# Forward transforms of a fused SSM convolution and feed-forward kernel: the small-tile matmuls' columns laid end to end over whole PSUM banks

## Chip, cores and metric

The kernel runs on one core of a Trainium2 chip, in one launch. The metric is the device time in microseconds: the median of three runs before the change is 1106.26 us (1106.08 to 1107.27). The engines are called PE (matmul), PEld (its weight loads), DVE (vector), ACT (scalar), POOL and SP (here mostly issuers of DMAs).

## What is computed

```python
x = A_u                                   # 1 x 2048 x 576
xn = layernorm(x)
return x + ssm_conv(xn, ...) + ffn(xn, w1, w2)

# ssm_conv: per channel d a response of 2048 taps, then a long convolution
dt = exp(log_dt);  P = exp(dt * A * l)                  # A complex, 576 x 128; l = 0..2047
K = real(sum_n C * P * (dt * B))                        # response, 576 x 2048
y = irfft(rfft(pad(u)) * rfft(pad(K)))[:2048] + u * Dskip
# ffn
out = silu(xn @ w1) @ w2                                # 576 -> 4608 -> 576
```

## The kernel before, in words

Two streams of work share the engines. The main stream is the feed-forward (`ffn`): for each half of the rows, for nine chunks of w1 and w2 and two blocks of 512 rows, `up` multiplies 128 columns of w1 into a bank of PSUM (L343 to L345; ACT applies SiLU on L351 and casts on L352, DVE forms the low part on L354) and `down` multiplies back with w2 (L369; DVE adds each bank to the running sum, L373). Operands are split into a high and a low part, so that three matmuls take the place of one. DVE and ACT also split the weights (L305, L328; L303, L326).

The side stream is the convolution: a first part makes the response and stores it to HBM (`d1k`), and a transform of the inputs (`d1u`); then `spectral` does the rest of the forward transforms, the products and most of the way back; `tail` reads its result (`d2`) for a last transform and adds it to the outputs. `weave` (L33) threads the side stream into the main one: a generator of the side yields a number between 0 and 1 (`marks` on L963 places `spectral` between 0.597 and 0.86), and its next piece is emitted when the feed-forward has come so far. Within that, the kernel's planner (L1133) orders each engine's queue by what it reckons to be ready; `tc.high_priority()` puts an instruction ahead, and `behind(ins)` forbids that an instruction is placed ahead of `ins` on the same engine.

`spectral` works on 16 pairs of frequencies, p = 0 to 15, each with a response operand and an input operand of 128 rows by two parts by 576 columns:

- `load_k`, `load_u`, `load_m` issue from POOL the loads of the response (five DMAs, L761 and L763), the input (L754) and the matrices (L771, L774).
- `halves` (L777): three operations of DVE make the two operands of the response (tile `k`, one buffer) from the loaded `kw` (two buffers).
- `visit` (L787): one operand is transformed by matmuls of 64 rows by 32 columns on eight small tiles of the array (two row groups, four column groups), L796. Its result is four banks of PSUM, [row group, column half], of which each holds 288 of 512 columns. One set of four banks (`psb`) serves all visits and `back`. There are 32 visits, a response and an input for each pair.
- `clear` (L813): ACT copies the four banks out in two copies of 576 columns (L817).
- `response` and `inputs` (L802, L819): after the response's visit ACT makes the swapped copies `kb` and `ka` (L808 to L810); after the input's visit DVE makes the complex products and their low parts (L827 to L834), ACT the high parts (L833).
- `back` (L836): twelve matmuls of 128 by 128 (L847), two copies out, two stores to `d2` from POOL (L852).

The loop of L877 emits for each p, a step of the stage each: the next response, the next input, `back`.

Of the kernel before, what the change touches and what calls it, by code (L numbers as in the profile page):

```python
# [19 lines left out]
P = 128  # L20
# [23 lines left out]
def kernel(  # L44
# [699 lines left out]
    def spectral():  # L744

        uv = d1u.rearrange("(m p r) d -> p r m d", m=2, r=P)
        kv = d1k.rearrange("(m p r) d -> p r m d", m=2, r=P)
        cwt = kl.tile([P, 16, 3], F32, name="cwt", bufs=1)
        nc.sync.dma_start(cwt, cw)
        us, ks, mats, kab, ys = {}, {}, {}, {}, {}  # L750

        def load_u(p):
            t = kl.tile([P, 2, D], F32, tag="u", name="u")
            nc.gpsimd.dma_start(t, uv[p])  # L754
            us[p] = t

        def load_k(p):
            if p > 15:
                return
            w = kl.tile([P, 3, D], F32, tag="kw", name="kw")  # L760
            nc.gpsimd.dma_start(w[:, 0:2], kv[p])  # L761
            for r in range(4):
                nc.gpsimd.dma_start(w[32 * r:32 * r + 32, 2], kv[p, 32 * (r ^ 1):32 * (r ^ 1) + 32, 1])  # L763
            ks[p] = w

        def load_m(p, i):
            if p > 15:
                return
            if i:
                t = kl.tile([P, 2, 2, P], F32R, tag="mm", name="mm")  # L770
                nc.gpsimd.dma_start(t, cm23[:, p, 1:].rearrange("r (k w) c -> r k w c", w=2))  # L771
            else:
                t = kl.tile([P, P], F32, tag="m2", name="m2")
                nc.gpsimd.dma_start(t, cm23[:, p, 0])  # L774
            mats[p, i] = t

        def halves(p):  # L777
            if p > 15:
                return
            w, t = ks[p], kl.tile([P, 2, D], F32, tag="k", name="k", bufs=1)  # L780
            ks[p] = t
            c = cwt[:, p]
            nc.vector.scalar_tensor_tensor(w[:, 2], w[:, 2], c[:, 0:1], w[:, 1], op0=ALU.mult, op1=ALU.add)
            for m in range(2):
                nc.vector.scalar_tensor_tensor(t[:, m], w[:, 2], c[:, 1 + m:2 + m], w[:, 0], op0=ALU.mult, op1=ALU.add)  # L785

        def visit(p, t, name):  # L787

            banks = psb.tile([P, 2, 2, 512], F32, tag="psb", name=name)
            last = pins["pe"]  # L790
            for n, (h, g) in enumerate(((0, 1), (0, 0), (1, 1), (1, 0))):
                gs = slice(64 * g, 64 * g + 64)
                for o in range(4):
                    os = slice(32 * o, 32 * o + 32)
                    with tc.high_priority(), behind(last):
                        last = nc.tensor.matmul(banks[os, g, h, :HD], mats[p, 0][gs, os], t[gs, o % 2, h * HD:(h + 1) * HD],  # L796
                                                start=True, stop=True, tile_position=(64 * g, 32 * o),
                                                skip_group_check=True).ins
            pins["pe"] = last
            return banks  # L800

        def response(p):  # L802

            kas = [kl.tile([P, D], F32, tag="ka", name="ka") for _ in range(2)]
            clear(visit(p, ks.pop(p), "pk"), kas)
            for g in range(2):
                ka, kb = kas[g], kl.tile([P, D], F32, tag="kb", name="kb")
                nc.scalar.mul(kb[:64], ka[64:], -1.0)  # L808
                nc.scalar.copy(kb[64:], ka[64:])
                nc.scalar.copy(ka[64:], ka[:64])  # L810
                kab[2 * p + g] = ka, kb

        def clear(banks, dsts):  # L813

            with tc.high_priority():
                for g in range(2):
                    nc.scalar.copy(dsts[g].rearrange("p (h d) -> p h d", h=2), banks[:, g, :, :HD])  # L817

        def inputs(p):  # L819

            uts = [kl.tile([P, D], F32, tag="ut", name="ut") for _ in range(2)]
            clear(visit(p, us.pop(p), "pu2"), uts)
            for g in range(2):
                ka, kb = kab.pop(2 * p + g)
                y = kl.tile([P, D], F32, tag="y", name="y", bufs=1)
                y2 = kl.tile([P, D], F32, tag="y2", name="y2", bufs=1)
                nc.vector.tensor_mul(y, uts[g], ka)  # L827
                nc.vector.tensor_mul(y2[:64], uts[g][64:], kb[:64])
                nc.vector.tensor_mul(y2[64:], uts[g][:64], kb[64:])  # L829
                nc.vector.tensor_add(y, y, y2)  # L830
                ys[2 * p + g] = [kl.tile([P, D], F32R, tag=n, name=n, bufs=2) for n in ("yh", "yl")]
                yh, yl = ys[2 * p + g]
                nc.scalar.copy(yh, y)  # L833
                nc.vector.tensor_sub(yl, y, yh)  # L834

        def back(p):  # L836
# [3 lines left out]
            for g in range(2):  # L840
                mk = mats[p, 1][:, g]
                parts = ys.pop(2 * p + g)
# [8 lines left out]
            for g in range(2):  # L851
                nc.gpsimd.dma_start(d2.rearrange("(p k) d -> k p d", k=32)[2 * p + g], yos[g])  # L852

        def load_u2(p):
            if p < 16:
                load_u(p)
# [280 lines left out]
```

## Time and profile before

| | |
|---|---|
| median of three runs | 1106.26 us |
| the profiled execution | 1106.58 us |
| its span, first to last instruction | 1104.8 us |
| granted clock of PE, mean | 1.000 |
| first visit, last matmul of `back` | 671.8 us, 976.7 us |
| small-tile matmuls of the visits, two groups (response, input) | 512 + 512 instructions |
| DMA share in the stage from 669 to 985 us | 0.49 |

A row of a timeline gives the start and the length in microseconds, engine, line, operation, the tile written and the tiles read, rows x columns of the stationary operand, the moving operand's shape and how many were merged into the row; in brackets stands the engine's idle time before it and what ended it. Matmuls are pipelined: what one costs is the distance between starts, not its length. A row of a table of stretches has start and end, length, the busy time (instructions) of PE, PEld, DVE, ACT and POOL, the granted clock, DMA share and GB/s. A row of groups has busy time, mean ns of one, idle time before and its releasers.

### The profile page before, as it was taken

To read this page: it belongs to the slowest core of one execution; us is meant where nothing else is said; L and a number is where in the kernel's file an instruction comes from. 1 tells how busy PE (TensorE), PEld (TensorE's weight loads), DVE (VectorE), ACT (ScalarE), POOL (GpSimd) and SP (SyncE) were. 2 spreads that over 40 slices of the span, in tenths; PEclk is the share of its full clock that TensorE was granted. 3 is DMA by queue.
4 is the path that set the end of the run, shared out by engine and by line. 5 is a ranking of instruction groups with operands and counts; after the bars stand their busy time and mean duration, and the time that the engine had idled before them with its cause. 6 is when DMAs were issued, how large, how long until landed. Compare 5 with 4: busy or idle time off the path is not lost.

```text
span 1104.8 us, 23941 instructions
## 1 busy us (share of the span) xinstructions
PE 1095.5 (99%) x9807; PEld 961.4 (87%) x9807; DVE 891.6 (81%) x1431; ACT 659.5 (60%) x1030; POOL 136.2 (12%) x241
## 2 busy tenths in 40 slices
PE   9999999999999999999999999999999999999998
PEld 7999998999889898999989988788878878899887
DVE  7799899999999999989999836786868768653343
ACT  4565457676776776767766644766666656732220
POOL 1100000000000000011000023323232231000011
PEclk9999999999999999999999999999999999999999
DMA  9745512524253425265754166555546453248563
GB/s 265 208 123 155 150 58 62 121 72 118 85 108 107 99 76 137 62 157 154 198 150 96 55 143 211 163 160 173 166 145 188 151 168 122 67 144 209 135 173 107
DMA packets 174142, 150.23 MB, mean 136 GB/s; under 512 B 112288, under 2 KB 143792, under 8 KB 173904
## 3 DMA queue, kind: packets, MB, share of 16 engines
q1 hardware_dynamic: 156544, 93.77, 32.9%
q0 software_dynamic: 16736, 54.07, 15.6%
q8 instruction: 77, 1.26, 0.5%
q10 hardware_dynamic: 752, 0.85, 0.3%
q14 instruction: 33, 0.27, 0.1%
HBM read 104.13 MB, written 44.61 MB: 135 GB/s over the span
## 4 chain that ended last, share of the span: by engine, by line
PE 80%; DVE 10%; DMA 4%; ACT 2%; POOL 1%; issue 1%; DVEq 0%; ACTq 0%; POOLq 0%
PE po L369 35%; PE ph L343 30%; PE kp L708 3%; DMA kw<-d1k 3%; PE ph L344 3%; PE ph L345 2%; PE z L723 2%; DVE y L829 1%; PE pb L847 1%; DVE y L830 1%; PE pu L171 1%; DVE k L785 1%; DVE acc L373 1%; POOL kw L763 1%; DVE y L827 1%
## 5 line engine op out<-in xcount | busy, mean ns | idle before, releaser
L369 PE MATMUL po<-w2h,gh 128*128 128x288 f32 x1152 | 340.2, 297 | 2.2 <-DVE acc L373 2.1
L369 PE MATMUL po<-w2l,gh 128*128 128x288 f32 x1152 | 337.2, 295 | 0.0
L369 PE MATMUL po<-w2h,gl 128*128 128x288 f32 x1152 | 336.4, 296 | 0.2 <-DVE gl L354 0.2
L369 PEld LDWEIGHTS po<-w2h,gh 128*128 128x128 f32 x1152 | 215.7, 188 | 19.9 <-issue 8.4
L369 PEld LDWEIGHTS po<-w2l,gh 128*128 128x128 f32 x1152 | 215.5, 188 | 6.7 <-issue 1.9
L369 PEld LDWEIGHTS po<-w2h,gl 128*128 128x128 f32 x1152 | 214.9, 188 | 2.9 <-issue 0.9
L351 ACT ACTIVATE gf<-ph 128x512 f32<-128x512 f32 (+1 forms) x146 | 85.8, 588 | 186.9 <-PE ph L345 168.7
L354 DVE TENSOR_TENSOR gl<-gf,gh 128x512 fp32r<-128x512 f32 (+1 forms) x148 | 98.6, 671 | 87.3 <-ACT gh L352 86.7
L373 DVE TENSOR_TENSOR acc<-po,acc 128x288 f32<-128x288 f32 x288 | 126.0, 451 | 47.6 <-PE po L369 46.0
L343 PE MATMUL ph<-xh,w1h 128*128 128x512 f32 (+1 forms) x584 | 159.5, 389 | 0.0
L343 PE MATMUL ph<-xh,w1l 128*128 128x512 f32 (+1 forms) x584 | 159.2, 387 | 0.0
L343 PE MATMUL ph<-xl,w1h 128*128 128x512 f32 (+1 forms) x584 | 159.0, 387 | 0.0
L343 PEld LDWEIGHTS ph<-xl,w1h 128*128 128x128 f32 x584 | 107.0, 188 | 22.0 <-issue 1.4
L343 PEld LDWEIGHTS ph<-xh,w1l 128*128 128x128 f32 x584 | 106.7, 188 | 20.3 <-issue 0.5
L343 PEld LDWEIGHTS ph<-xh,w1h 128*128 128x128 f32 x584 | 103.6, 188 | 17.9 <-issue 0.9
L352 ACT CAST gh<-gf 128x512 fp32r<-128x512 f32 (+1 forms) x148 | 89.3, 610 | 19.4 <-PE po L369 16.4
L174 POOL DMA_DIRECT2D d1u<-u x32 | 17.4, 545 | 462.3 <-ACT u L173 460.4
L667 ACT ACTIVATE c<-th 128x1040 f32<-128x1040 f32 x36 | 38.7, 1075 | 46.0 <-DVE th L666 46.0
L833 ACT CAST yh<-y 128x576 fp32r<-128x576 f32 x32 | 21.5, 673 | 74.2 <-DVE y L830 71.0
L665 ACT ACTIVATE c<-th,magic 128x1040 f32<-128x1040 f32 x36 | 42.1, 1169 | 26.4 <-DVE C L688 23.3
L305 DVE TENSOR_TENSOR w1l<-w1r,w1h 128x640 fp32r<-128x640 f32 x72 | 57.0, 819 | 0.2
L344 PE MATMUL ph<-x,w1h 128*128 128x512 f32 (+1 forms) x146 | 56.6, 388 | 0.0
(195 smaller groups left out, 1757.7 us busy)
## 6 DMA issues: line engine op xcount, KB each, us to landing
w2r<-in_B_w_dram SPq DMA_DIRECT2D x72, 288.0 KB, 3.8
w1r<-in_B_w_dram SPq DMA_DIRECT2D x35, 512.0 KB, 3.9
d1u<-u POOLq DMA_DIRECT2D x32, 288.0 KB, 3.0
d1k<-stage SPq DMA_DIRECT2D x36, 256.0 KB, 5.1
u<-d1u POOLq DMA_DIRECT2D x16, 576.0 KB, 4.6
kw<-d1k POOLq DMA_DIRECT2D x16, 576.0 KB, 4.6
d<-yo POOLq DMA_DIRECT2D x32, 288.0 KB, 3.0
ys<-d SPq DMA_DIRECT2D x32, 288.0 KB, 6.0
```

The source lines that it names most:

```text
L305: pins["w1l"] = nc.vector.tensor_sub(l1, src, h1).ins
L343: nc.tensor.matmul(ph, w[:, kt, :], v[:, kt, a:e], start=n + kt == 0, stop=False)
L344: nc.tensor.matmul(ph, h1[:, 4, :], x4[:, a:e], start=False, stop=False)
L345: pins["pe"] = nc.tensor.matmul(ph, l1[:, 4, :], x4[:, a:e], start=False, stop=True).ins
L351: nc.scalar.activation(gf, ph, AF.Silu)
L352: pins["gh"] = nc.scalar.copy(gh, gf).ins
L354: pins["gl"] = nc.vector.tensor_sub(gl, gf, gh).ins
L369: pins["pe"] = nc.tensor.matmul(po[:, :HD], G[blk, t][g][:, js], W2[half, c, t][w][:, hs], start=n == 0, stop=n == 3 * FT - 1).ins
L373: nc.vector.tensor_add(acc[j][:, hs], po[:, :HD], acc[j][:, hs])
L665: nc.scalar.activation(c65, th, AF.Identity, bias=magic)
L667: nc.scalar.activation(c65, th, AF.Abs)
L708: mm = nc.tensor.matmul(dst, t[:, ch, :32], t[:, ch, 32:], start=begins and n == 0, stop=True, tile_position=(0, 32 * q), skip_group_check ...
```

## The change

The 32 operands (response 0, input 0, response 1, input 1, ...) are laid end to end, 576 columns each, and cut at every 512 columns, so that each visit fills its four banks wholly: 18 visits of 1024 columns for each row group, each with two to four pieces of up to three operands. A visit's pieces are 64 to 512 columns wide. ACT copies each piece out, both row groups at once, into tiles `ka` and `ut` that now hold both row groups of a pair. The swapped copies of the response are made after the visit in which the pair's input ends, in `products`, followed by the products of DVE, which now write in place into `kb` and `ut`. `halves` works in place in `kw`; the tile `k` is gone. The loads of the pair two on are issued right behind the visit that ends an operand; `halves` of a pair is emitted one visit after its buffer was freed, or in the same step where the next visit already needs it. `back` of a pair comes after the visit behind the one that ended its input. The small matrix `m2` has three buffers. The stage starts its first visit at 1.07 of its scale (1.05 before), with the loads of pair 1 moved up.

```diff
+        visits = [[] for _ in range((2 * D * NP + 1023) // 1024)]
+        for p in range(NP):
+            for kind in range(2):
+                c, at = 0, 2 * D * p + D * kind
+                while c < D:
+                    n = min(D - c, 512 - (at + c) % 512)
+                    visits[(at + c) // 1024].append((kind, p, c, n, (at + c) % 1024 // 512, (at + c) % 512))
+                    c += n
+        ends = [[(kind, p) for kind, p, c, n, _, _ in v if c + n == D] for v in visits]
...
         def halves(p):
...
-            w, t = ks[p], kl.tile([P, 2, D], F32, tag="k", name="k", bufs=1)
...
+                w, c = ks[p], cwt[:, p]
+                nc.vector.scalar_tensor_tensor(w[:, 2], w[:, 2], c[:, 0:1], w[:, 1], op0=ALU.mult, op1=ALU.add)
+                for m in range(2):
+                    nc.vector.scalar_tensor_tensor(w[:, 1 - m], w[:, 2], c[:, 1 + m:2 + m], w[:, 0],
+                                                   op0=ALU.mult, op1=ALU.add)
...
-        def visit(p, t, name):
-
-            banks = psb.tile([P, 2, 2, 512], F32, tag="psb", name=name)
+        def visit(v):
+
+            banks = psb.tile([P, 2, 2, 512], F32, tag="psb", name="pf")
             last = pins["pe"]
-            for n, (h, g) in enumerate(((0, 1), (0, 0), (1, 1), (1, 0))):
-                gs = slice(64 * g, 64 * g + 64)
-                for o in range(4):
-                    os = slice(32 * o, 32 * o + 32)
...
+            for kind, p, c, n, b, at in visits[v]:
+                for g in (1, 0):
+                    gs = slice(64 * g, 64 * g + 64)
+                    for o in range(4):
+                        os = slice(32 * o, 32 * o + 32)
+                        src = us[p][gs, o % 2] if kind else ks[p][gs, 1 - o % 2]
+                        with tc.high_priority(), behind(last):
+                            last = nc.tensor.matmul(banks[os, g, b, at:at + n], mats[p, 0][gs, os], src[:, c:c + n],
+                                                    start=True, stop=True, tile_position=(64 * g, 32 * o),
+                                                    skip_group_check=True).ins
             pins["pe"] = last
...
+            for kind, p, c, n, b, at in visits[v]:
+                held, tag = (uts, "ut") if kind else (kas, "ka")
+                if c == 0:
+                    held[p] = kl.tile([P, 2, D], F32, tag=tag, name=tag)
+                with tc.high_priority():
+                    nc.scalar.copy(held[p][:, :, c:c + n], banks[:, :, b, at:at + n])
+
+        def products(p):
+
+            ut, ka = uts.pop(p), kas.pop(p)
+            kb = kl.tile([P, 2, D], F32, tag="kb", name="kb", bufs=1)
             for g in range(2):
...
+                nc.scalar.mul(kb[:64, g], ka[64:, g], -1.0)
+                nc.scalar.copy(kb[64:, g], ka[64:, g])
+                nc.scalar.copy(ka[64:, g], ka[:64, g])
+            yield
             for g in range(2):
...
+                nc.vector.tensor_mul(kb[:64, g], ut[64:, g], kb[:64, g])
+                nc.vector.tensor_mul(kb[64:, g], ut[:64, g], kb[64:, g])
+                nc.vector.tensor_mul(ut[:, g], ut[:, g], ka[:, g])
+                nc.vector.tensor_add(ut[:, g], ut[:, g], kb[:, g])
+                yh, yl = (kl.tile([P, D], F32R, tag=n, name=n) for n in ("yh", "yl"))
+                nc.scalar.copy(yh, ut[:, g])
+                nc.vector.tensor_sub(yl, ut[:, g], yh)
...
         with behind(pins["gh"]):
             halves(0)
+        load_k(1)
+        load_m(1, 0)
+        load_u(1)
         load_m(0, 1)
...
+        yield 1.04
         halves(1)
...
+        load_m(2, 0)
+        steps = len(visits) + NP
...
+        for p in range(2, NP):
+            freed = (2 * D * (p - 2) + D - 1) // 1024
+            due.setdefault(min(freed + 1, 2 * D * p // 1024 - 1), []).append(p)
+        for v in range(len(visits)):
+            yield 1.07 + (2 - 1.07) * n / steps
+            n += 1
+            visit(v)
+            for kind, p in ends[v]:
+                if kind:
+                    load_u(p + 2)
+                    load_m(p + 3, 0)
+                else:
+                    load_k(p + 2)
+            done = [p for kind, p in ends[v] if kind]
+            for p in done:
+                for _ in products(p):
+                    pass
+            for p in due.get(v, ()):
+                halves(p)
+            for p in ready:
+                yield 1.07 + (2 - 1.07) * n / steps
+                n += 1
+                back(p)
                 load_m(p + 1, 1)
...
+            ready = done
```

More of the change, by code (lines that the diff above doesn't have):

```diff
@@ L761, in load_k @@
[L761 to L764, printed above, removed]
-        def load_m(p, i):
[L767 to L775, printed above, removed]
```

110 lines of the change are left out of this document (34 added, 76 removed).

## The prediction

> **What bounds the kernel now.** I read the page's busy table first, then the stretches, then the PE's own waits, then the timeline of one visit.
>
> ```profile
> span 1104.8 us, 23941 instructions
> ...
> PE 1095.5 (99%) x9807; PEld 961.4 (87%) x9807; DVE 891.6 (81%) x1431; ACT 659.5 (60%) x1030; POOL 136.2 (12%) x241
> ```
> ```profile
> 669.00:985.00 316.00, 313.65 (x2671) 261.80 (x2670) 234.56 (x361) 206.63 (x342) 80.64 (x144) 1.00 0.49 149
> 985.00:1105.00 120.00, 115.19 (x897) 100.31 (x896) 48.30 (x99) 24.27 (x42) 10.72 (x22) 1.00 0.62 161
> ```
> ```profile
> PE po L369 <- DVE acc L373: 2.1, 3, 0.7
> ```
>
> The first fence says that PE is busy for 99% of the span. A busy PE can hide overhead, so the stage of the change has to be read alone: 669 to 985 us, where PE is busy for 313.65 of 316 us at granted clock 1.00, DVE for 234.56 (74%), ACT for 206.63 (65%). The third fence has PE's waits in that stage: 2.1 us, for DVE's adds of the feed-forward. So PE is not waiting for the transform; it is full, and what changes the time here is the PE time that a visit costs, or a wait put into PE's queue. After 985 us PE is busy for 115.19 of 120 us, so a gain made earlier is carried to the end.
>
> ```profile
> 744.88 0.29 PE L369 MATMUL po<-w2l,gh 128*128 128x288 f32 x1
> 745.01 0.43 PE L369 MATMUL po<-w2h,gl 128*128 128x288 f32 x2
> 745.37 1.20 PE L796 MATMUL pk<-k,m 64*32 64x288 f32 x32
> 746.50 0.40 PE L369 MATMUL po<-w2h,gh 128*128 128x288 f32 x1
> 746.74 0.29 PE L369 MATMUL po<-w2l,gh 128*128 128x288 f32 x1
> ```
> ```profile
> 745.37 0.47 PE L796 MATMUL pk<-k,m 64*32 64x288 f32 x8
> ...
> 745.37 0.71 PE L796 MATMUL pk<-k,m 64*32 64x288 f32 x16
> ...
> 745.37 0.96 PE L796 MATMUL pk<-k,m 64*32 64x288 f32 x24
> ```
>
> These are one visit among feed-forward matmuls, and the same visit cut off by narrower windows. Feed-forward matmuls start 0.13 us apart, so the last one before the visit starts at 745.14. From there to 746.74 is 1.60 us, where two ordinary intervals would take 0.27: **a visit costs PE 1.33 us**. Inside it, 8, 16, 24 and 32 instructions take 0.47, 0.71, 0.96 and 1.20 us: each eight (one for each of the eight small tiles) take 0.243 us for 288 columns, 0.97 us for four eights. The other **0.36 us are fixed**: the switch into small tiles (0.10), out of them (0.11), and the fill and drain of the small tiles.
>
> **The change part by part.**
>
> ```profile
> L796 PE MATMUL pk<-k,m x512: 402/403/428, 671.8 to 955.6; 64*32 64x288 f32 x171
> ...
> L796 PE MATMUL pu<-u,m x512: 402/403/428, 678.9 to 961.3; 64*32 64x288 f32 x171
> ```
> ```profile
> L847 PE MATMUL pb<-yh,mm x128: 288/294/300, 699.7 to 976.7; 128*128 128x288 f32 x128
> ```
>
> *Matmuls.* Now: 1024 instructions, 32 a visit, 32 visits. After: 32 operands of 576 columns laid end to end, cut at every 512 columns, give 64 pieces (eight each of 512, 448, 384, 320, 256, 192, 128 and 64 columns) of 16 instructions: 1024 again, and 18,432 columns a row group, as now. Streaming stays at 32 x 0.97 = 31.1 us. Fixed: 32 x 0.36 = 11.5 us becomes 18 x 0.36 = 6.5 us. That is **5.0 us less on PE**, and all of it on the path.
>
> *Short pieces.* No visit shows a 64-column piece. The nearest other rows:
>
> ```profile
> 168.60 0.34 PE L708 MATMUL kp<-C 128*32 128x64 f32 x8
> ...
> 170.59 0.66 PE L369 MATMUL po<-w2h,gl 128*128 128x288 f32 x3
> ```
> ```profile
> 168.60:170.62 2.02, 2.02 (x128) 1.90 (x128) 1.00 0.04 8
> ```
>
> Here 128 instructions of 64 columns on four tiles take 1.99 us, 15.5 ns each. If that were a floor for each instruction, a piece of 16 would take at least 0.25 us, where 64 columns need 2 x 0.054 = 0.11 and 128 need 0.22: 0.14 + 0.03 us for each of eight, 1.4 us in all. The other end is nothing: inside the visit the first eight start within some 0.05 us (0.47 less the 0.43 of the longest one), 6 ns apart, and the four-tile row is itself near its streaming, 62 ns for a round of four against 54. I take 0.1 us, by the visit's row, and keep 1.4 for the range.
> [...]
>
> *Evictions, products, halves.*
>
> ```profile
> L667 ACT ACTIVATE c<-th 128x1040 f32<-128x1040 f32 x36 | 38.7, 1075 | 46.0 <-DVE th L666 46.0
> L173 ACT COPY u<-pu 128x288 f32<-128x288 f32 x64 | 24.3, 399 | 15.8 <-PE pu L172 15.8
> L817 ACT COPY ka<-pk 128x576 f32<-128x576 f32 x32 | 18.9, 640 | 3.3 <-PE pk L796 2.0 <-DVE y L827 1.3
> L809 ACT COPY kb<-ka 64x576 f32<-64x576 f32 x32 | 21.5, 671 | 0.4
> ```
> ```profile
> L373 DVE TENSOR_TENSOR acc<-po,acc 128x288 f32<-128x288 f32 x76 | 33.6, 452 | 7.0 <-PE po L369 6.6
> L354 DVE TENSOR_TENSOR gl<-gf,gh 128x512 fp32r<-128x512 f32 x39 | 26.7, 689 | 42.2 <-ACT gh L352 41.8
> L785 DVE SCALAR_TENSOR_TENSOR k<-kw,cwt 128x576 f32<-128x576 f32 x32 | 24.7, 812 | 0.0
> L829 DVE TENSOR_TENSOR y<-ut,kb 64x576 f32<-64x576 f32 x32 | 24.2, 756 | 0.5
> L305 DVE TENSOR_TENSOR w1l<-w1r,w1h 128x640 fp32r<-128x640 f32 x19 | 15.0, 821 | 0.1
> L328 DVE TENSOR_TENSOR w2l<-w2r,w2h 128x576 fp32r<-128x576 f32 x19 | 13.9, 752 | 0.0
> L783 DVE SCALAR_TENSOR_TENSOR kw<-kw,cwt 128x576 f32<-128x576 f32 x16 | 13.1, 817 | 12.1 <-DMA kw<-d1k 11.6 <-DVE y L829 0.2
> ```
>
> ACT evicts response and inputs with 64 copies of 576 columns now and with 64 copies of 128 to 1024 columns after, the same columns in all; from 399 and 640 ns a copy costs about 0.16 us and 0.84 ns a column, so the sum stays and the longest is about 1.0 us (the 1040-column row: 1.075). The six half copies of an operand pair (0.67 each, 4.0 us) move from behind the response's visit to behind the end of the inputs'. DVE does the same 13 operations a pair, 10 x 0.756 + 2 x 0.812 + 0.817 = 10.0 us, now in place. All of this is cost nothing, hidden under PE's 313.65 us while DVE and ACT have 26% and 35% of the stage free. If that cover went, PE would wait for the feed-forward's own work in the same in-order queues (L373, L354 on DVE, L351 and L352 on ACT).
>
> *Loads and waits.* POOL issues the same transfers. The load of the response two pairs on now waits for the visit that has read the buffer, not for DVE's halves:
>
> ```profile
> 749.57 0.72 POOL L761 DMA_DIRECT2D kw<-d1k  x1 [5.73 <-DVE k L785]
> 750.28 1.99 POOL L763 DMA_DIRECT2D kw<-d1k  x4
> ```
> ```profile
> DMA to landing us min/median/max: 3.1/4.2/9.4
> ```
>
> The last line is the landing of the transfers of `kw`. Behind the load in POOL's queue stand the input's load, the small matrix (a third buffer) and later the stores of back; POOL already sits through 5.73 us of such a wait, and is busy for only 80.64 of 316 us. The chain: visit 2.0, issue 2.7, landing 4.2 (at most 9.4), three halves 2.4 us: 11.3, at most 16.5. The time for it: 48 visits and backs now span 671.8 to 976.7; 34 start some 6 us later (1.07 of the stage's scale for 1.05) and save 5, so they come (305 - 11) / 33 = 8.9 us apart. For four pairs (6, 7, 14, 15) the freeing visit and the needing one are neighbours with one back between, 17.8 us; for the other ten there is a visit more. A visit that holds columns of both kinds waits for the later of them; behind it on PE stands all of the feed-forward. Since back follows three steps (26.7 us) after the visit, the longer chain of evictions, half copies, products (about 16 us of ACT and DVE) has room. I cost these at nothing. The first loads are only moved up in POOL's queue, ahead of a first visit that comes later. The single `kb` tile is free again a whole visit before its next use.
>
> Sum: 1104.8 - 5.0 + 0.1 = 1099.9 of span. The profiled execution took 1106.58, 1.78 more than its span, and stands 0.32 above the median: 1099.9 + 1.8 - 0.3 = **1101.4 us** beside 1106.26.
>
> **The rivals.**
>
> ```profile
> 671.77 0.67 PE L796 MATMUL pk<-k,m 64*32 64x288 f32 x2
> ...
> 673.29 1.20 PE L796 MATMUL pk<-k,m 64*32 64x288 f32 x30
> ```
> ```profile
> 899.22 0.40 PE L369 MATMUL po<-w2h,gh 128*128 128x288 f32 x1 [0.72 <-DVE acc L373]
> ```
> ```profile
> 747.07 0.75 DVE L830 TENSOR_TENSOR y<-y,y 128x576 f32<-128x576 f32 x1
> 747.73 1.54 DVE L785 SCALAR_TENSOR_TENSOR k<-kw,cwt 128x576 f32<-128x576 f32 x2
> 749.19 0.75 DVE L834 TENSOR_TENSOR yl<-y,yh 128x576 fp32r<-128x576 f32 x1
> ```
>
> 1. **It doesn't do what it says: visits fall apart.** The first visit now is two, 2 and 30 instructions with feed-forward between, since its order only forbids overtaking. Each break pays the fixed 0.36 us again. A visit now has up to three operands to wait for; nine breaks give back 3.2 us: 1104.6. Against it: the timeline shows no other visit broken so.
> 2. **A floor for each small instruction**, as under the short pieces: 1.3 us more than I take by the four-tile row, 1102.7. With a floor f, the pieces of 64, 128 and 192 columns lose 8 x (48 f - 0.65 us); the gain of 5.0 is gone at f = 27 ns, and the time is then that of before. Against it: the two rows above, 6 and 15.5 ns. [...]
> 3. **Slower: the halves come too late.** They stand in the code behind the ten products of the same step. If DVE keeps that order, the products start 6.2 us after the visit's start (visit 1.9, evictions 2.3, three half copies 2.0), and 7.56 + 2.44 us at the 72% that the feed-forward leaves (89.2 of 316 us are its own: 33.6 + 26.7 + 15.0 + 13.9) end at 20.1. It decides at 17.8: PE then stands 2.3 us at a visit. At the four narrow pairs that is 9.2 us, 1110.6; at all fourteen 32, 1133. Against it: the last fence shows DVE taking the halves of a later pair ahead of the last product of an earlier one, and PE's queue can put feed-forward ahead of a late visit.
> 4. **Bunching: DVE's or ACT's longer runs hold up L373.** Such a wait costs 0.72 us and some 0.1 for the refill; there are three. Nine in place of three cancel the gain; one for each of 16 pairs adds 13 x 0.8 = 10.4: 1111.8. For it: evictions, half copies and products now follow one visit; against it: no single operation but one copy gets longer.
>
> **How the numbers follow.** Forecast 1101.4: 0.62, since PE is full and the fixed cost is the same in every visit. Rival 1: 0.09; rival 2: 0.06; rival 3: 0.13; rival 4: 0.10. The forecast's own range is 1097.8 (the three waits and the broken visit's 0.8 us gone too) to 1104. A measurement of this kernel can tell about 0.2%, 2.2 us. Faster: 0.62 + 0.03 + 0.04 of rivals 1 and 2 = 0.69; same: 0.06 + 0.02 of these, 0.06 of mild cases of 3 and 4 = 0.14; slower: 0.17. The range goes from 1097.4 up to 1110.6, the four narrow pairs, leaving out some 0.12 above and 0.04 below.
>
> **What would show it.** Right: 18 groups of 48 to 64 small-tile instructions, L369 resuming as it does now, the group's rows summing to some 37 us; PE's waits in the stage at about 2 us; last back some 5 us earlier or level. [...] Rival 1: more than 18 groups. Rival 3: PE idle ahead of a visit with the halves or the kw load as releaser. Rival 4: more rows of PE behind L373. Wrong altogether if PE's busy share in the stage falls below 98%.

## The result and the profile after

| | before | after |
|---|---|---|
| median of six runs each, us | 1106.17 (1105.54 to 1107.27) | 1113.49 (1112.63 to 1114.27) |
| ratio | | 1.0065 [1.0052, 1.0078] |
| span of the profiled execution, us | 1104.8 | 1112.4 |
| PE busy in the stage, 669 to 985 us | 313.65 of 316 | 306.44 of 316 |
| last matmul group of `back`, us | 976.7 | 967.9 |

Forecast was 1101.4 us, faster; measured is 7.3 us slower, outside the range.

First the page of the changed kernel (span, busy times, granted clock in 40 slices), then the stretch of the stage.

```profile
span 1112.4 us, 23927 instructions
...
PE 1095.9 (99%) x9807; PEld 965.5 (87%) x9807; DVE 889.0 (80%) x1431; ACT 659.7 (59%) x1030; POOL 137.1 (12%) x241
...
PEclk9999999999999999999999999999999998999999
```
```profile
669.00:985.00 316.00, 306.44 (x2625) 259.37 (x2624) 230.84 (x357) 203.92 (x337) 80.20 (x143) 0.99 0.50 152
```

PE's busy time over the span is 99% as before and tells nothing. In the stage it fell by 7.2 us (99.3% to 97.0%), so PE now waits for something; one of the 40 clock slices reads 8. That 7.2 is so near the loss of 7.3 us is chance: the account below adds up shorter visits, waits and a stretch at half clock, in which PE counts as busy. Its own waits in the stage:

```profile
PE po L369 <- DVE acc L373: 8.1, 6, 3.3
PE pb L846 <- ACT ut L813: 1.1, 2, 0.9
PE pf L804 <- ACT yo L851: 0.2, 1, 0.2
```

A row has total, times and the longest. The visits (L804) wait for 0.2 us in all: no row has halves or a load holding up a visit. What is held up is the feed-forward, behind DVE's adds (L373): 8.1 us in place of 2.1. So the next view is what DVE waits for, after and then before:

```profile
DVE kw L788 <- DMA kw<-d1k: 29.4, 8, 8.5
```
```profile
DVE kw L783 <- DMA kw<-d1k: 11.6, 5, 5.4
```

DVE stands 29.4 us at the first operation of the halves, waiting for the response's load, up to 8.5 us at once; before it was 11.6. Everything behind it in DVE's queue stands too. The two rows belong together: five of PE's waits for DVE's adds are over 0.3 us (1.32, 1.98, 0.67, 0.71 and 3.30 us, ending at 699, 757, 767, 801 and 932 us), and before each of them DVE had worked without a break over 0.3 us since such a wait for a load (2.73, 8.52, the same 8.52, 3.93 and 3.35 us).

**One such place.** The changed kernel around 743 us: SP's and POOL's DMA issues, the stretches, DVE, and PE.

```profile
742.36 1.66 SPq L315 DMA_DIRECT2D w2r<-in_B_w_dram  x3
```
```profile
743.16 0.72 POOL L771 DMA_DIRECT2D kw<-d1k  x1 [3.15 <-DVE w2l L328]
743.87 1.98 POOL L773 DMA_DIRECT2D kw<-d1k  x4
745.84 0.75 POOL L766 DMA_DIRECT2D u<-d1u  x1
```
```profile
746.00:748.00 2.00, 2.00 (x13) 1.75 (x12) 0.00 (x0) 1.93 (x4) 1.13 (x2) 1.00 0.92 318
748.00:750.00 2.00, 2.00 (x17) 2.00 (x16) 0.00 (x0) 1.95 (x3) 0.00 (x0) 1.00 0.96 287
```
```profile
743.58 0.68 DVE L354 TENSOR_TENSOR gl<-gf,gh 128x512 fp32r<-128x512 f32 x1
752.78 0.82 DVE L788 SCALAR_TENSOR_TENSOR kw<-kw,cwt 128x576 f32<-128x576 f32 x1 [8.52 <-DMA kw<-d1k]
753.63 0.75 DVE L825 TENSOR_TENSOR kb<-ut,kb 64x576 f32<-64x576 f32 x1
...
756.84 0.46 DVE L373 TENSOR_TENSOR acc<-po,acc 128x288 f32<-128x288 f32 x1
```
```profile
757.35 0.40 PE L369 MATMUL po<-w2h,gh 128*128 128x288 f32 x1 [1.98 <-DVE acc L373]
```

The load is issued 0.37 us behind the end of the visit's first piece, which read its buffer last (742.45 to 742.79; the bracket names one of DVE's w2l operations, which ended at about the same time), together with three pieces of w2 (288 KB each) and the input's load (576 KB). The response itself is 576 + 288 KB. That is 2304 KB, 2.36 MB, and at the 287 to 318 GB/s of the stretches it takes an estimated 7.8 us; the halves start 9.6 us after the issue. DVE finished its last earlier work at 744.26 and then idles for 8.52 us, though products (L825, for the first of which ACT had finished the copies by 747.27) and the add of L373 stand behind: none of them goes ahead of the halves. When the load lands, halves and products of some 4 us still go first, and PE idles 1.98 us at 757.35.

**The longest.** PE of the same kernel behind the visit at 926 us, then the stretch behind it, then DVE ahead of it.

```profile
928.22 0.42 PE L804 MATMUL pf<-kw,m 64*32 64x128 f32 x16
931.94 0.61 PE L369 MATMUL po<-w2h,gh 128*128 128x288 f32 x1 [3.30 <-DVE acc L373]
```
```profile
932.00:937.00 5.00, 5.00 (x21) 5.00 (x22) 2.12 (x4) 3.61 (x6) 0.00 (x0) 0.50 0.28 77
```
```profile
919.28 0.82 DVE L788 SCALAR_TENSOR_TENSOR kw<-kw,cwt 128x576 f32<-128x576 f32 x1 [3.35 <-DMA kw<-d1k]
...
931.44 0.81 DVE L373 TENSOR_TENSOR acc<-po,acc 128x288 f32<-128x288 f32 x2
```

DVE first waited 3.35 us for a load, then worked without a break from 919.28 to the add at 931.44; PE stood for 3.30 us. Afterwards its matmuls start 0.24 us apart instead of 0.13, at a granted clock of 0.50, until about 937.4: 22 matmuls x 0.11 = 2.4 us more.

**The account.** Distances between the starts of PE's matmuls, summed over the whole trace (a visit with its two switches; a stall is a distance over 0.06 us beyond the ordinary one, half clock included): visits 43.3 to 39.7 us, stalls in the stage 3.6 to 14.6, the tail 0.2 more; everything else is equal to 0.1. -3.6 + 11.0 + 0.2 = +7.6 of span, as measured.

### The profile page after: what moved, and what is told of

It reads as the page before. It is cut to its first block, busy times and chain, and to the rows that moved or that the text cites. A ratio compares the mean times of both kernels' runs of the same rounds, so it can differ in the third digit from the quotient of the medians.

```text
span 1112.4 us, 23927 instructions
## 1 busy us (share of the span) xinstructions
PE 1095.9 (99%) x9807; PEld 965.5 (87%) x9807; DVE 889.0 (80%) x1431; ACT 659.7 (59%) x1030; POOL 137.1 (12%) x241
## 4 chain that ended last, share of the span: by engine, by line
PE 84%; DVE 6%; DMA 4%; ACT 3%; issue 1%; POOL 1%; SPq 0%; DVEq 0%; ACTq 0%
PE po L369 37%; PE ph L343 31%; PE kp L708 3%; DMA kw<-d1k 3%; PE ph L344 3%; PE ph L345 3%; PE z L723 2%; PE pb L846 2%; PE pf L804 1%; PE pu L171 1%; PE py L955 1%; DMA acc<-in_A_u_dram 1%; PE pu L172 1%; DVE kw L790 1%; DVE ut L827 1%
## 5 line engine op out<-in xcount | busy, mean ns | idle before, releaser
L351 ACT ACTIVATE gf<-ph 128x512 f32<-128x512 f32 (+1 forms) x146 | 86.0, 589 | 192.8 <-PE ph L345 175.2
L373 DVE TENSOR_TENSOR acc<-po,acc 128x288 f32<-128x288 f32 x288 | 126.1, 451 | 67.2 <-PE po L369 66.2
L354 DVE TENSOR_TENSOR gl<-gf,gh 128x512 fp32r<-128x512 f32 (+1 forms) x148 | 98.5, 670 | 72.8 <-ACT gh L352 72.6
L345 PE MATMUL ph<-x,w1l 128*128 128x512 f32 (+1 forms) x146 | 56.5, 387 | 0.0
```

Source lines behind the costliest of these rows:

```text
L345: pins["pe"] = nc.tensor.matmul(ph, l1[:, 4, :], x4[:, a:e], start=False, stop=True).ins
L351: nc.scalar.activation(gf, ph, AF.Silu)
L354: pins["gl"] = nc.vector.tensor_sub(gl, gf, gh).ins
L373: nc.vector.tensor_add(acc[j][:, hs], po[:, :HD], acc[j][:, hs])
```

## The experiments

**Theory A**: the loss is the late load of the response. In the kernel before, three tiles (two `kw`, one `k`) carry it, and DVE's halves free a `kw` early; now only the visit frees it, the load goes out right behind the visit, DVE meets the unfinished load in order, and the adds of the feed-forward behind it hold up PE. **Theory B**: bunching. The work of a pair comes in larger lumps (18 visits, with evictions, copies, products and halves behind each), and the lumps themselves hold up L373, load or not. The stalls below are those of the account above (us in the stage); "waits" is DVE's idle time at the halves for which a load is named; in three_kw, three_kw_spread, three_kw_ease and three_kw_ease2 4.3, 2.7, 8.5 and 6.3 us more have no releaser in the profile. Each ratio is to runs of `before` made beside that kernel's (their medians are 1105.57 to 1106.58), so a difference of under 1 us between two rows' times means little. Stalls and waits are those of the one profiled execution; that of three_kw_ease took 1109.25 us, the longest of its eleven, that of mm_one 1112.03, the shortest of its five.

| kernel | time, us | ratio to before | visits | stalls | waits |
|---|---|---|---|---|---|
| before | 1106.17 | | 43.3 | 3.6 | 11.6 |
| after | 1113.49 | 1.0065 [1.0052, 1.0078] | 39.7 | 14.6 | 29.4 |
| a_noload | 1103.33 | 0.9979 [0.9970, 0.9988] | 39.5 | 4.2 | 2.1 |
| b_noload | 1103.07 | 0.9975 [0.9966, 0.9983] | 43.3 | 0.0 | 2.0 |
| three_kw | 1104.79 | 0.9992 [0.9983, 1.0001] | 39.5 | 5.6 | 14.2 |
| late_halves | 1111.11 | 1.0048 [1.0035, 1.0061] | 40.0 | 11.2 | 16.6 |
| mm_one | 1113.71 | 1.0077 [1.0064, 1.0091] | 39.7 | 12.4 | 29.2 |
| spread_products | 1110.58 | 1.0039 [1.0026, 1.0052] | 41.1 | 9.0 | 27.4 |
| three_kw_spread | 1108.87 | 1.0025 [1.0015, 1.0034] | 39.5 | 8.7 | 17.6 |
| b_in_place | 1111.85 | 1.0052 [1.0040, 1.0065] | 43.5 | 8.7 | 18.2 |
| late_u | 1113.73 | 1.0057 [1.0044, 1.0071] | 39.7 | 13.8 | 28.7 |
| three_kw_ease | 1106.57 | 1.0005 [0.9996, 1.0013] | 39.8 | 9.6 | 23.2 |
| b_three_kw | 1104.87 | 0.9986 [0.9977, 0.9995] | 43.3 | 1.2 | 21.4 |
| noload_spread | 1101.59 | 0.9964 [0.9952, 0.9977] | 39.5 | 2.6 | 2.6 |
| three_kw_late | 1107.55 | 1.0016 [1.0008, 1.0025] | 39.5 | 7.6 | 7.2 |
| three_kw_ease2 | 1107.65 | 1.0018 [1.0009, 1.0027] | 39.5 | 7.4 | 21.9 |

**a_noload and b_noload: the loads taken away.** In both kernels the response's buffers of pairs 0 and 1 are used again for all later pairs, so that these two serve for the time alone: the response of pairs 2 to 15 is left out.

```diff
-            if p < NP:
+            if 2 <= p < NP:
+                ks[p] = ks[p - 2]
+            elif p < NP:
                 w = ks[p] = kl.tile([P, 3, D], F32, tag="kw", name="kw")
```

> The changed kernel, leaving out the loads of the response for pairs 2 to 15 (the buffers of pairs 0 and 1 are used again), all operations of DVE, ACT and PE kept. Theory A (late load: with the halves written in place, a buffer is free only when the visit has read it, so the next response lands late, DVE waits in order at the halves, 29.4 us in all, and the feed-forward's adds behind it come late): DVE never waits for kw, PE's stalls behind L373 fall from 8.1 us to 2 or 3, no clock drop; about 1102.5 us (1101 to 1104.5). Theory B (bunching: ten products, three halves and six half copies behind one visit hold up the adds, whatever the load does): stalls stay, 1110 us or more.

> The kernel before, leaving out the same loads: the control of the run above. Both theories: DVE's waits for kw (11.6 us) cost PE at most 1 us there, so 1105 to 1106.2 us. Theory A then puts the changed kernel without loads 3 to 4 us below this one (the visits' gain as the trace shows it), theory B 4 us or more above it.

PE's wait for DVE in the stage of a_noload; b_noload has no wait of PE there at all.

```profile
PE po L369 <- DVE acc L373: 1.6, 2, 0.9
```

The loads cost the changed kernel 10.2 us (9.5 by the ratios) and the kernel before about 2.5, where at most 1 was expected. But a_noload isn't below b_noload, where 3 to 4 us less was expected: 3.8 us less for visits, 4.2 us more of stalls. So theory A names most of the loss, and a remainder as large as the visits' gain is left, for B or for ACT (PE's last longer wait of a_noload, 0.79 us at 864 us, is behind ACT's copies). One thing in a_noload isn't in b_noload: halves written in place wait for the visit that reads the same buffer, 6.1 us of DVE in three waits. The last of them ends at 829 us, and PE has no stall over 0.25 us between 736 and 862 us, so the remainder isn't theirs.

**three_kw: the load a pair earlier.** The third part of the response gets a buffer of its own (`kx`, loaded behind the halves of the pair before), the other two parts three buffers; the matrices of `back` one buffer, for room.

```diff
-                w = ks[p] = kl.tile([P, 3, D], F32, tag="kw", name="kw")
-                nc.gpsimd.dma_start(w[:, 0:2], kv[p])
+                ks[p] = kl.tile([P, 2, D], F32, tag="kw", name="kw", bufs=3)
+                nc.gpsimd.dma_start(ks[p], kv[p])
...
-                    load_k(p + 2)
+                    load_k(p + 3)
```

> The changed kernel with three buffers of the response in place of two, so that each load is issued one pair earlier; the third part of the load has one buffer of its own, loaded behind the halves of the pair before; to make room mm has one buffer. Theory A: DVE's wait for the load falls from 29.4 us to under 5, PE's stalls in the stage from 14.6 to 5 or less; 1103 us (1101.5 to 1105). Theory B: 1111 us or more, since DVE's work is as bunched as before.

PE's wait for DVE in the stage:

```profile
PE po L369 <- DVE acc L373: 2.5, 5, 0.8
```

With all its transfers done, it is 8.7 us (8.1 by the ratios) faster than the changed kernel, and level with the kernel before. So the loss hangs on when the load is issued, not on its being made. The time came as expected, DVE's wait did not: 14.2 us are left where under 5 were expected, and PE's stalls fell to 5.6 all the same. mm_one is the control for the single buffer of the matrices:

```diff
-                    t = kl.tile([P, 2, 2, P], F32R, tag="mm", name="mm")
+                    t = kl.tile([P, 2, 2, P], F32R, tag="mm", name="mm", bufs=1)
```

> The changed kernel with one buffer of mm in place of two and nothing else: the control of three_kw, where that went along. Theory A (the gain of three_kw is the earlier load): no change, 1113.5 us (1111 to 1115). Rival (POOL's queue, in which mm waits up to 21 us for back with the loads behind it, made the difference): 1105 to 1108 us.

No difference in the time, as expected.

**b_in_place: the buffer change alone.** The kernel before, 32 visits, with the halves written in place in `kw` and the tile `k` gone.

```diff
-            w, t = ks[p], kl.tile([P, 2, D], F32, tag="k", name="k", bufs=1)
-            ks[p] = t
-            c = cwt[:, p]
+            w, c = ks[p], cwt[:, p]
...
-                nc.vector.scalar_tensor_tensor(t[:, m], w[:, 2], c[:, 1 + m:2 + m], w[:, 0], op0=ALU.mult, op1=ALU.add)
+                nc.vector.scalar_tensor_tensor(w[:, 1 - m], w[:, 2], c[:, 1 + m:2 + m], w[:, 0], op0=ALU.mult, op1=ALU.add)
```

> The kernel before with the halves written in place in kw and the tile k gone: that one part of the change alone, with 32 visits. The load is then freed by the visit here too, but in this order its halves are due almost a whole pair later. Theory A as first put (freeing by the visit makes the load late) by itself: 1108 us or more, DVE's waits for kw well over 11.6 us. A with the spacing (only 18 visits with two pairs in each leave so little between freeing and need): no change, 1105.6 us (1104.5 to 1106.5).

DVE's wait at the halves, and PE's waits, in the stage:

```profile
DVE kw L781 <- DMA kw<-d1k: 18.2, 7, 3.8
```
```profile
PE po L369 <- DVE acc L373: 2.7, 5, 0.9
PE po L369 <- ACT gh L352: 1.6, 1, 1.6
PE ph L343 <- ACT gf L351: 0.9, 1, 0.9
```

Two of DVE's operations a pair write to another tile, and PE has not one instruction more or less: 5.7 us slower. So the part of the change that saves a tile loses most of the time by itself, without the 18 visits. The load is indeed issued later, by 17 to 23 us from pair 4 on, and DVE waits longer for it. But PE's waits don't stand behind these: of its eight over 0.3 us only the second shortest, 0.39 us at 695 us, follows DVE work that began with a wait for a load. Three follow ACT's work, and before the other four DVE had been idle for 4.2 to 5.3 us with ACT as releaser. One of them, DVE's row and PE's:

```profile
775.63 0.69 DVE L354 TENSOR_TENSOR gl<-gf,gh 128x512 fp32r<-128x512 f32 x1 [5.27 <-ACT gh L352]
```
```profile
788.02 0.40 PE L369 MATMUL po<-w2h,gh 128*128 128x288 f32 x1 [0.90 <-DVE acc L373]
```

Between the two DVE works without a break, through the three halves of a pair among products and weight splits, and the add for which PE waits comes last. Here the later load seems to cost by moving the halves into the lump, not by standing unfinished in the queue; no run leaves that lump out, so it is argued and not shown.

**b_three_kw: the same cure for the kernel before**, with its tile `k`.

```diff
-            w = kl.tile([P, 3, D], F32, tag="kw", name="kw")
-            nc.gpsimd.dma_start(w[:, 0:2], kv[p])
+            w = kl.tile([P, 2, D], F32, tag="kw", name="kw", bufs=3)
+            nc.gpsimd.dma_start(w, kv[p])
...
-            load_k(p + 3)
+            load_k(p + 4)
```

> The kernel before with its 32 visits, the response in three buffers and its third part in a buffer of its own, loaded a pair earlier (the matrices of back in one buffer, for room). Theory A: the load of the response costs the kernel before 2.5 us (leaving it out gave 1103.1), so that here DVE's waits for kw fall from 11.6 us to 4 or less and the time to 1103.0 to 1104.5, level with three_kw, which would mean that the 18 visits are worth nothing beside an earlier load. Rival: the kernel before's load was early enough, its waits of PE come from elsewhere: 1105.3 to 1106.5, and three_kw keeps 1 us over it.

DVE's waits in the stage, and PE's:

```profile
DVE gl L354 <- ACT gh L352: 39.2, 16, 7.4
DVE kx L789 <- DMA kx<-d1k: 19.3, 7, 4.8
DVE kx L789 <- DMA kw<-d1k: 2.1, 1, 2.1
```
```profile
PE po L369 <- ACT gh L352: 0.5, 1, 0.5
```

The time came as expected, the reason not: DVE waits longer for loads than in the kernel before (21.4 us), but PE only 0.5. Here the wait falls where DVE is ahead anyway (it idles 39.2 us for ACT at L354; the changed kernel has 14.7). So a sum of DVE's waits doesn't give the price. That is decided by what stands behind the wait, and here the products come in smaller lumps. This kernel is faster than the one before by 0.14% and level with three_kw: as built, without the tile `k`, the 18 visits brought nothing beside an earlier load.

**Where the halves stand, and the lumps.** late_halves emits the halves behind the step's `back`; spread_products does so with the products of the second row group; three_kw_spread joins the latter to three_kw.

```diff
-            for p in due.get(v, ()):
-                halves(p)
...
+            for p in due.get(v, ()):
+                with behind(pins["gl"]):
+                    halves(p)
             ready = done
```

> The changed kernel with the halves emitted after the step of back, some 9 us later, and kept behind the latest low part of the feed-forward (L354): nothing else moved. Theory A: the load has landed by then, DVE's wait falls to under 8 us; 1105 us (1103 to 1108), less sure than with three buffers, since the next visit may wait for the halves. Theory B: less of a bunch right behind the visit, but the products are still ten in a row: 1110 us or more.

```diff
-            for p in done:
-                for _ in products(p):
-                    pass
+            todo = [products(p) for p in done]
+            for g in todo:
+                next(g)
+                next(g)
...
+            for g in todo:
+                with behind(pins["gl"]):
+                    next(g)
             ready = done
```

> The changed kernel with the products of the second row group moved behind the step of back, so that DVE's ten operations come in two fives some 9 us apart; loads untouched. Theory A (late load): DVE still waits about 25 to 30 us for kw, 1112 to 1114 us. Theory B (bunching) as the main cause: 1106 us or less. B as a remainder of some 4 us, which is what the run without loads left: 1109 to 1111 us.

> Three buffers of the response and the products in two parts. If the load and the bunching are the two causes, PE's stalls in the stage fall from 5.6 us with three buffers alone to 2 or 3, and the 3.8 us that the visits give show: 1101.5 to 1103 us, under both kernels. If the remainder has another cause: as three_kw, 1104.8 us.

late_halves was a miss: the waits fell only to 16.6, since the planner still put the halves 6.4 to 10.2 us behind the load's issue in 8 of 14 pairs. PE's own waits in the stage did fall, from 9.4 to 5.5 us, but its granted clock was 0.50 from 701.27 to 708.10 and from 889.00 to 892.41 us, which at 0.24 us a matmul in place of 0.13 costs an estimated 4 to 5 us. spread_products gained 2.9 us with DVE's waits as they were: bunching has a part of its own. three_kw_spread was a miss in sign, 4.1 us slower than three_kw, with new waits for ACT (L351, 1.2 us) among its stalls: the two cures don't add.

**late_u: the input's load emitted later.**

```diff
-                if kind:
+                if kind and (2 * D * (p + 2) + D) // 1024 == v + 1:
                     load_u(p + 2)
                     load_m(p + 3, 0)
...
+                if (2 * D * (p + 2) + D) // 1024 > v:
+                    load_u(p + 2)
+                    load_m(p + 3, 0)
             ready = done
```

> The changed kernel, but the load of the input two pairs on and that of the small matrix are emitted behind the pair's back, a step later, wherever the next visit does not need them yet (13 of 16 pairs); the response's load stands alone behind its visit. Theory A in its form 'the response's load lands late because it shares the DMA engines with what is issued beside it': landing of kw falls from a median of 6.0 us to 5 or less, DVE's waits at the halves for kw from 29.4 to 18 us or less, PE's idle time behind DVE's adds (8.1 us) to 4 or less, time 1107 to 1110 us. Rival, theory A in its other form (the halves stand in DVE's queue at the reckoned landing, and the load comes 1 to 4 us later than reckoned whatever lies beside it): landing may fall by 1 us, waits stay at 22 us or more, time 1111 to 1114. Theory B (bunching alone): no change, 1113.

POOL's issues at the place of the longest wait (7.8 us), and DVE's waits:

```profile
744.64 0.72 POOL L771 DMA_DIRECT2D kw<-d1k  x1 [3.15 <-DVE w2l L328]
...
747.32 0.75 POOL L766 DMA_DIRECT2D u<-d1u  x1
```
```profile
DVE kw L788 <- DMA kw<-d1k: 28.7, 8, 7.8
```

Nothing changed, and the rows say why that decides nothing: in all 14 pairs the input's load stands in POOL's queue where it stood, 1.3 us ahead of the response's, 2.7 us behind it, or far off. The edit moved no input load against the response's. The changed kernel's own trace says more. In six pairs the input's load goes out 1.3 us ahead of the response's, and the first transfer of the response (576 KB) lands after 6.4 to 7.3 us; in the kernel before, the input's load follows 2.7 to 4.3 us behind, and in 12 of 13 pairs it lands after 4.3 to 4.8 us. The longest landings, 7.9 and 8.2 us, have the input's load 2.7 us behind and pieces of w1 or w2 within 1 us. So neighbours go with a late landing; no run moved them alone, and what the later issue adds was not told apart.

**What the visits are worth bare.** noload_spread is a_noload with the spread products.

> The changed kernel without the response's loads of pairs 2 to 15 (as a_noload, so the result is not the reference's), and the products of the second row group emitted behind the pair's back. Theory: what a_noload has left, 4.2 us of PE stalls in the stage, is theory B's bunching of halves and products ahead of the feed-forward's adds on DVE; spread, stalls in the stage fall to 1.5 us or less and the time to 1100 to 1101.5 us: the 18 visits' gain would stand there bare. Rival: the stalls come from ACT's run of evictions and copies, or from the order as such: 3 us or more stay, time 1102.5 to 1105.

PE's only wait in the stage has a_noload's row to the digit, 1.6 us behind DVE's adds in two waits.

Stalls 2.6, not 1.5 or less; 1101.59 us, 1.7 below a_noload and 1.5 below b_noload (the ratios' intervals overlap; the profiled spans, 1099.6 beside 1101.3 and 1101.5 us, agree). Only here, with loads and lumps both eased, do the 18 visits show in the time, with less than half of their 3.8 us. What went are a_noload's stalls at 857 to 881 us, the longest of them behind ACT; the two waits behind DVE's adds, which the edit was aimed at, stayed. So this run doesn't show that a lump on DVE makes the remainder.

**Two tries for a faster kernel.** three_kw_ease and three_kw_ease2 set the first visits further apart; three_kw_late puts the halves of three_kw behind `back`, with the edit of late_halves.

```diff
-        steps = len(visits) + NP
+        steps = len(visits) + NP + 3
...
+            n += not ready
             for p in ready:
```

> As three_kw (response loaded into three buffers, a pair earlier), and in a step with a visit and no back (three of them, two at the start of the stage) the scale moves on by one step more, so that visits stand two steps apart from the first on; steps are 8.1 us in place of 8.9. What three_kw has left (1104.8 us, PE stalls of 5.6 us in the stage) is by theory B the crowding of the three first visits' halves and products at 671 to 711 us: then stalls between 690 and 712 us fall under 1 us, the sum in the stage to 3 us or less, time 1101.5 to 1103.5. Rival: the work is only pushed into shorter steps and the stalls move to later stretches: sum 5 us or more, time 1104.3 to 1107.

```diff
-        steps = len(visits) + NP
+        steps = len(visits) + NP + 2
...
-            yield 1.07 + (2 - 1.07) * n / steps
+            yield 1.05 + (2 - 1.05) * n / steps
...
+            n += v < 2
```

> As three_kw, with the two steps more only at the start of the stage and the first visit at 1.05 of the scale, so that the other steps stay nearly as long as in three_kw (8.3 us against 8.7). Theory B: the crowding at 690 to 712 us goes (as it did in three_kw_ease) and nothing comes later: stalls in the stage 3 us or less, time 1101.5 to 1103.5. Rival: any change of the steps' places makes stalls of its own elsewhere: 4.5 us or more, 1104 to 1107.

> As three_kw, with the due halves emitted behind the step's back and not ahead of its adds in DVE's queue. Theory A and B together: DVE's waits at the halves fall from 14.2 us to 5 or less, the stalls in the stage from 5.6 to 3 us or less, time 1101.5 to 1103.5. Rival: the single buffer of the third part is then loaded later by as much and is waited for in place of kw (waits 10 us or more), or the halves land on the products of the next pair: 1104.5 to 1109.

All three missed. The profiled execution of three_kw_ease, 2.7 us above its median, has no stall over 0.25 us before 793 us, so three_kw's stalls at 698 to 736 went with the crowd of first visits; but it has others at 794, 854 to 857 and 881 to 885, where also a weight's cast is late (PE's two longest rows of waits in the stage):

```profile
PE po L369 <- ACT w2h L326: 2.3, 1, 2.3
PE po L369 <- DVE acc L373: 2.2, 4, 1.3
```

three_kw_late halves DVE's waits (14.2 to 7.2) and has 2 us more of stalls. With 18 visits, each of these placements moved the stalls rather than removing them.

## Why the prediction was wrong

- **PE is full, changes there carry over**: right. The stage's -3.6 and +11.0 us arrive in the span with 0.2 us more from the tail.
- **Fixed cost of a visit**: right that fewer visits cost less, and the gain smaller: -3.6 us in place of -5.0. What the 0.36 us hold beside the two switches was the prediction's reading; no run shows it apart. Three visits of the changed kernel:

```profile
783.93 0.77 PE L804 MATMUL pf<-kw,m 64*32 64x320 f32 x16
784.50 1.18 PE L804 MATMUL pf<-u,m 64*32 64x192 f32 x32
785.47 0.42 PE L804 MATMUL pf<-kw,m 64*32 64x128 f32 x16
785.82 0.40 PE L369 MATMUL po<-w2h,gh 128*128 128x288 f32 x1
...
816.05 1.20 PE L804 MATMUL pf<-kw,m 64*32 64x512 f32 x32
817.05 1.12 PE L804 MATMUL pf<-u,m 64*32 64x448 f32 x16
818.10 0.40 PE L369 MATMUL po<-w2h,gl 128*128 128x288 f32 x1
```
```profile
742.45 0.34 PE L804 MATMUL pf<-kw,m 64*32 64x64 f32 x16
742.58 1.18 PE L804 MATMUL pf<-u,m 64*32 64x448 f32 x32
743.55 0.90 PE L804 MATMUL pf<-kw,m 64*32 64x384 f32 x16
744.38 0.72 PE L343 MATMUL ph<-xh,w1h 128*128 128x512 f32 x2
```

  From the first row of each to the feed-forward's: 1.89, 2.05 and 1.93 us, where all have 1024 columns a row group. Those with a piece of 64 columns (the second has one between 512 and 448) take 0.04 to 0.16 us more. The eights of 64 columns start 0.055 to 0.08 us apart, where the forecast reckoned 0.054; the piece behind them starts late. In all some 0.9 us, where 0.1 was taken, inside the bound of 1.4; at 7 to 10 ns an instruction, there is no floor near the 27 ns of rival 2. With both switches a visit without such a piece costs 2.08 us, which is the forecast's 37.5 us over 18. Most of the rest of the 1.4 us is the first visit, whose break now costs 1.17 us in place of 0.80.
- **Rival 1**: only the first visit is broken, as before. Rival 2: a part of 1 us, above.
- **Evictions, products, halves at nothing, hidden**: wrong in part. a_noload keeps 4.2 us of stalls where b_noload has none, and spread_products, its loads as late, is 2.9 us faster than the changed kernel. A share of the stage (74% busy) can't say that an in-order queue is never late.
- **The step that failed: "Loads and waits ... I cost these at nothing."** The chain from a visit through the load to the next visit was reckoned at 11.3 us, at most 16.5, against 17.8 us, and that held: no visit waits for it (the steps are 9.0 us on average, though the first visit starts at 671.5 us and not 6 us later than before). But it asked only whether the visit would be late. The waiting instruction is not the visit; it is DVE's halves, and behind it in DVE's queue stand the adds L373 for which PE waits. The load goes out 1.0 to 16.6 us later than before in 12 of 14 pairs, and beside others; DVE reaches the halves before it has landed in 8 of the 14. From the load's issue to the halves it is 6.7 to 12.6 us, before 5.8 to 8.0. Of the 11 us of stalls 10 go with the loads (a_noload, 14.6 to 4.2) and 9 with having them earlier (three_kw, 5.6). The landing of `kw`, after (before: 4.2 in the median, 9.4 at most):

```profile
DMA to landing us min/median/max: 3.2/6.0/10.3
```

  The prediction had the row that warned of it, 11.6 us of DVE at L783 for this very load, and did not ask what the later issue would add to it. The page of before had another that it did not read, the chain that ended last by line; the same line of b_three_kw has no kw in it.

```profile
PE po L369 35%; PE ph L343 30%; PE kp L708 3%; DMA kw<-d1k 3%; PE ph L344 3%; PE ph L345 2%; PE z L723 2%; DVE y L829 1%; PE pb L847 1%; DVE y L830 1%; PE pu L171 1%; DVE k L785 1%; DVE acc L373 1%; POOL kw L763 1%; DVE y L827 1%
```

  3% of 1104.8 us are some 33 us of that chain on the response's loads: a sign that a later load could be felt. It isn't a price, since leaving the loads out gave only 2.5 us (b_noload), and the changed kernel's chain has 3% of kw too.
- **Rival 3** (halves too late, PE idle at a visit) had the halves right and the place wrong: PE never waited at a visit for them. **Rival 4** (L373 held up) had the place and the sign right, 1111.8, at a chance of 0.10, with another cause, so that its number is near is luck: it reckoned 13 more waits of 0.8 us, and there are six in all, up to 3.30 us, one of which the half clock followed, 2.4 us.
- **What would show it**: "wrong altogether if PE's busy share in the stage falls below 98%" was the right test; it is 97.0%.

Open: the split of the late landing between late issue and neighbours; what stalls PE in b_in_place; and why the 18 visits' lumps stall PE in each placement tried. b_three_kw, with longer waits and hardly a stall, shows that a wait of DVE alone isn't enough; the lump behind it is only argued to be the other half, from spread_products.

## What to carry to other kernels

Where an edit saves a buffer, ask what frees the buffer afterwards, when its load then goes out, and which instruction meets the unfinished load first. Then look at everything behind that instruction in its queue: here DVE stood 29.4 us at the halves, and the price was paid by PE, which waited 8.1 us for DVE's adds, not by the visits that read the load, none of which waited for it. A transfer that stands in the chain that ended last, even with 3%, is worth this question before it is issued later.

## What the runs showed of the hardware

With some of PE's stops its granted clock fell to 0.50, with others it stayed at 1.00. After 3.30 us of idling in the changed kernel the clock was 0.50 from 932 to 937 us; it had been 1.00 up to 930.70, and was 0.50 from there, 1.24 us before PE went on, to 937.52. In late_u 3.29 us at 932.36 were followed by the same, in mm_one 3.26 us at 932.30 were not:

```profile
932.70:936.00 3.30, 3.30 (x16) 3.30 (x16) 1.05 (x2) 3.20 (x5) 0.00 (x0) 0.52 0.41 115
```
```profile
932.70:936.00 3.30, 3.30 (x25) 3.26 (x25) 2.00 (x4) 3.20 (x5) 0.00 (x0) 1.00 0.33 108
```

The first row is late_u (clock 0.52, 16 matmuls), the second mm_one (1.00, 25). So the length of a stop alone doesn't tell its outcome: 3.26 us kept the clock, and in spread_products a stop of 1.83 us was followed by half clock:

```profile
757.09 0.40 PE L369 MATMUL po<-w2h,gh 128*128 128x288 f32 x1 [1.83 <-DVE acc L373]
```
```profile
758.43:761.84 3.41, 3.41 (x65) 1.69 (x49) 3.41 (x7) 0.16 (x1) 2.54 (x5) 0.50 0.22 49
```

In late_halves a stop of 1.83 us that ended at 699.90 was followed by a clock of 0.50 from 701.27 to 708.10; in the changed kernel one of 1.98 us that ended at 757.35 was not followed by any (the clock was 1.00 from 750 to 766 us). What decides it, these runs don't show.
